# A second level of seven block products inside gate and up of an already Strassen-like MLP

## Chip, cores, metric

One Trainium2 chip, one core of it. The metric is the device time of one execution in microseconds (us). A ratio of two kernels is the mean time of one's fast runs over the mean time of the other's fast runs of the same rounds, so it is not quite the ratio of the medians that are quoted.

Engines: PE is the matrix engine (TensorE), DVE the vector engine, ACT the scalar engine, POOL the GpSimd engine. PEld in the profile is PE's loading of weights. SBUF is the on-chip memory that all engines read; PSUM holds PE's results, in banks of 512 f32 columns.

## The reference

Two layers, each a linear attention block (A) and a bilinear gated MLP (B), with a residual around both. Only B matters here:

```python
def _B_ref(x, w_gate, w_up, w_down):      # x (1, 2048, 1024), F = 3584
    g = jnp.einsum("bsd,df->bsf", x, w_gate)
    u = jnp.einsum("bsd,df->bsf", x, w_up)
    h = g * u
    return jnp.einsum("bsf,fd->bsd", h, w_down)
```

## The kernel before

All tensors of B lie in one big on-chip array, the "arena", so the profile calls every operand `arena` and every accumulator `ps` (PSUM). A small planner records each instruction with the bytes it reads and writes, and adds the semaphore waits.

B already replaces 2x2 block products by the seven products of the Strassen-Winograd scheme. A *unit* is a pair of 128-column feature tiles of gate (m = 0) or of up (m = 1), over 1024 tokens. Its seven products take 4 matmuls of 128x128 by 128x512 each, 28 instead of 32. There are 28 units in a *pass* (14 of gate, 14 of up), and two passes in each of the two layers: passes 1 to 4. After each pass comes the down projection of the same tokens.

```python
xs = {"1": (raw[:, 0:4, 0:128], rraw, xblk(0, s0), r_xblk(0, s0)),      # weights, activations
      "2": (raw[:, 4:8, 0:128], rraw, xblk(1, s0), r_xblk(1, s0)),
      "3": (sv[:, 3], rs[3], xblk(1, s0 + 512), r_xblk(1, s0 + 512)),
      "4": (raw[:, 4:8, 128:256], rraw, T4, rT[2]),
      "5": (sv[:, 0], rs[0], T1, rT[0]), ... }
def pe(q, bank, start):
    w, rw, x, rx = xs[q]
    P.add("pe", lambda e: [e.matmul(psb(bank), w[:, k, :], x[:, k, :], start=(start and k == 0), stop=(k == 3),
                                    skip_group_check=True) for k in range(4)], rd=rw + rx, pwr=[bank])
def fin(b, bank, ti):                                                   # a finished block of gate or up
    ...
    if ti is None:
        if m == 0: P.add("act", ... AF.Copy ...)                        # gate: ACT copies it out
        else:      stt(hv[:, j, :], psb(bank), SG, g4[b], gr, hr, prd=[bank], op1=ALU.mult)
    elif m == 0:
        stt(g4[b], psb(bank), SG, tm[ti][0], tm[ti][1], gr, prd=[bank])
    else:                                                               # up: add, then multiply with gate
        stt(ut, psb(bank), SG, tm[ti][0], tm[ti][1], ur, prd=[bank])    # DVE, one input in PSUM, one in SBUF
        tt(hv[:, j, :], ut, g4[b], ALU.mult, ur + gr, hr)               # DVE, both inputs in SBUF
...
```

`stt` is a DVE scalar_tensor_tensor, `tt` a DVE tensor_tensor.

## Time and profile before

The time is 1497.7 us (median of 4 runs, 1495.4 to 1498.2).

The first lines are from the page of the kernel before: the span, busy time with its share of the span, the chain of waits that ended last by engine, and the costliest group (busy us, mean ns of one, then the idle time before it).

```profile
span 1495.1 us, 17704 instructions
...
PE 1479.0 (99%) x6925; PEld 660.1 (44%) x6990; DVE 913.9 (61%) x1530; ACT 449.2 (30%) x732; POOL 216.0 (14%) x239
...
PE 91%; DVE 3%; DMA 3%; issue 1%; POOL 1%; ACT 1%; SPq 0%; ACTq 0%
...
L912 PE MATMUL ps<-arena 128*128 128x512 f16 x3136 | 679.0, 379 | 1.9 <-DVE arena L613 1.3
```

PE is busy throughout and the chain is PE: 679.0 us / 3136 = 216.5 ns per gate/up matmul. The mean of 379 ns in the line is one matmul from start to end; they overlap, and their starts in the trace lie 216 ns apart.

The next answer is the view of stretches, one row for each of the four passes, from the first gate/up matmul to the last: length, busy us of each engine with the number of instructions, granted PE clock, DMA share, GB/s.

```profile
core 0: us, PE busy (x) PEld busy (x) DVE busy (x) ACT busy (x) POOL busy (x), PEclk, DMA share, GB/s
243.10:415.70 172.60, 171.18 (x791) 73.42 (x791) 129.18 (x288) 66.70 (x113) 2.37 (x6) 1.00 0.83 253
499.00:669.50 170.50, 170.45 (x791) 73.44 (x791) 83.27 (x143) 66.11 (x112) 6.31 (x16) 1.00 0.72 207
983.70:1154.90 171.20, 170.58 (x790) 73.42 (x790) 74.25 (x125) 67.73 (x114) 2.36 (x6) 1.00 0.56 170
1238.20:1408.80 170.60, 170.55 (x791) 73.51 (x791) 68.69 (x111) 66.11 (x112) 0.00 (x0) 1.00 0.56 177
```

PE fills all four. DVE fills 75% of pass 1 and 40 to 49% of the others; POOL does next to nothing. The DVE line is its largest group of tensor_tensor with 512 elements and both inputs in SBUF, from the groups by line with shapes kept apart:

```profile
L610 DVE TENSOR_TENSOR arena<-arena 128x512 f16<-128x512 f16 x140 | 59.5, 425 | 4.8
```

### The profile page before, as it was taken

The page shows a single profiled execution, that of the slowest core. Times are in us where ns is not written, and L with a number is a line of the kernel's source. Part 1 is how long each engine was busy: PE and PEld are TensorE (multiplying, and loading weights), DVE is VectorE, ACT ScalarE, POOL GpSimd, SP SyncE. Part 2 cuts the span into 40 slices and gives each one's busy share as a digit, 9 for nine tenths or more (in the row PEclk, how much of TensorE's full clock was granted, in tenths as well). Part 3 has the DMA queues.
Part 4 walks back from the last instruction along what each step waited for, and adds up shares of the span by engine and source line. Part 5 has one row for each costly group of instructions (what it writes and reads, how often), then busy time and mean ns, then how long its engine had stood idle before and what let it go on. Part 6 is the DMA issues. An engine that isn't in the chain of part 4 may idle for free.

```text
span 1495.1 us, 17704 instructions
## 1 busy us (share of the span) xinstructions
PE 1479.0 (99%) x6925; PEld 660.1 (44%) x6990; DVE 913.9 (61%) x1530; ACT 449.2 (30%) x732; POOL 216.0 (14%) x239
## 2 busy tenths in 40 slices
PE   8999999999999999999999999999999999999999
PEld 4444444444444444444444444444444444444444
DVE  7986978777656463445488678764344553434453
ACT  3332355333300234330023314543333003334200
POOL 4544621000000010000044345310000000000000
PEclk9999999999999999999999999999999999999999
DMA  6134656799854896544466247555554455555352
GB/s 225 36 92 111 149 132 150 229 285 278 262 203 151 260 257 193 176 164 148 141 184 178 80 93 186 146 139 172 178 173 163 163 190 186 177 175 177 131 172 99
DMA packets 300643, 254.40 MB, mean 170 GB/s; under 512 B 102288, under 2 KB 266384, under 8 KB 300560
## 3 DMA queue, kind: packets, MB, share of 16 engines
q1 hardware_dynamic: 300560, 253.27, 57.4%
q8 instruction: 55, 0.90, 0.3%
q14 instruction: 28, 0.23, 0.0%
HBM read 195.04 MB, written 34.60 MB: 154 GB/s over the span
## 4 chain that ended last, share of the span: by engine, by line
PE 91%; DVE 3%; DMA 3%; issue 1%; POOL 1%; ACT 1%; SPq 0%; ACTq 0%
PE ps L912 43%; PE ps L1035 23%; PE ps L672 15%; PE ps L754 7%; PE ps L840 2%; DMA arena<-in_B_w_down_dram 1%; DVE arena L610 1%; DVE arena L412 1%; DMA arena<-arena 1%; DMA arena<-in_A_wqkv_dram 1%; POOL arena L701 1%; PE ps L766 0%; PE ps L794 0%; SPq L386 0%; POOL arena L417 0%
## 5 line engine op out<-in xcount | busy, mean ns | idle before, releaser
L912 PE MATMUL ps<-arena 128*128 128x512 f16 x3136 | 679.0, 379 | 1.9 <-DVE arena L613 1.3
L613 DVE SCALAR_TENSOR_TENSOR arena<-ps,arena 128x512 f16<-128x512 f32 (+2 forms) x480 | 327.2, 689 | 470.6 <-PE ps L912 161.8
L912 PEld LDWEIGHTS ps<-arena 128*128 128x128 f16 (+1 forms) x3136 | 291.4, 98 | 388.2 <-ACT arena L916 36.0
L1035 PE MATMUL ps<-arena 128*128 128x512 f16 (+1 forms) x1548 | 338.0, 379 | 1.1
L1035 PEld LDWEIGHTS ps<-arena 128*128 128x128 f16 x1568 | 153.5, 98 | 185.0
L672 PE MATMUL ps<-arena 128*128 128x512 bf16 x1003 | 222.1, 379 | 4.6 <-DMA arena<-in_A_wqkv_dram 1.6
L916 ACT ACTIVATE arena<-ps 128x512 f32<-128x512 f32 x224 | 133.7, 597 | 291.1 <-PE ps L912 288.9
L610 DVE TENSOR_TENSOR arena<-arena 128x512 f16<-128x512 f16 (+3 forms) x360 | 197.9, 574 | 18.3 <-DMA arena<-in_B_w_down_dram 8.3
L672 PEld LDWEIGHTS ps<-arena 128*128 128x128 f16 x1024 | 99.6, 98 | 122.4 <-DMA arena<-in_A_wqkv_dram 2.1
L558 ACT ACTIVATE arena<-ps 128x512 f32<-128x512 f32 x128 | 76.4, 597 | 232.6 <-PE ps L672 218.4
L938 ACT COPY ps<-ps 128x512 f32<-128x512 f32 x112 | 63.9, 570 | 204.3 <-PE ps L912 203.7
L754 PE MATMUL ps<-arena 128*128 128x512 bf16 x500 | 114.6, 379 | 0.6
L840 PE MATMUL ps<-arena 128*128 128x512 bf16 x502 | 110.8, 379 | 3.2 <-ACT ps L834 2.7
L415 POOL TENSOR_SCALAR arena<-arena 128x1 f32<-128x1 f32 x64 | 20.7, 323 | 598.7 <-DVE arena L414 598.7
L412 DVE BATCH_NORM_STATS2 arena<-arena 128x6 f32<-128x512 bf16 x128 | 88.1, 689 | 13.1 <-DMA arena<-in_A_x_dram 6.7
L701 POOL TENSOR_TENSOR arena<-arena 128x1024 f16<-128x1024 f32 x32 | 79.8, 2493 | 90.3 <-DVE arena L699 83.7
L926 ACT ACTIVATE arena<-ps 128x512 f16<-128x512 f32 x112 | 66.9, 597 | 84.5 <-PE ps L912 84.5
L561 DVE SCALAR_TENSOR_TENSOR arena<-ps,arena 128x512 bf16<-128x512 f32 x128 | 88.5, 692 | 4.4
L684 POOL TENSOR_TENSOR arena<-arena 128x512 f32<-128x512 f32 x60 | 74.6, 1248 | 87.0 <-DVE arena L561 85.6
L559 DVE TENSOR_SCALAR arena<-arena 128x512 f32<-128x512 f32 x128 | 65.9, 515 | 27.7 <-ACT arena L558 26.6
L840 PEld LDWEIGHTS ps<-arena 128*128 128x128 f16 x512 | 49.8, 98 | 63.9 <-ACT ps L834 4.4
L754 PEld LDWEIGHTS ps<-arena 128*128 128x128 f16 x512 | 49.3, 98 | 55.7
(45 smaller groups left out, 381.9 us busy)
## 6 DMA issues: line engine op xcount, KB each, us to landing
arena<-s_scratch SPq DMA_DIRECT2D x84, 512.0 KB, 3.3
arena<-in_B_w_gate_dram SPq DMA_DIRECT2D x56, 512.0 KB, 4.2
arena<-in_B_w_up_dram SPq DMA_DIRECT2D x56, 512.0 KB, 3.9
arena<-t_scratch SPq DMA_DIRECT2D x32, 896.0 KB, 4.8
arena<-in_B_w_down_dram SPq DMA_DIRECT2D x24, 896.0 KB, 4.6
s_scratch<-arena SPq DMA_DIRECT2D x28, 512.0 KB, 6.9
arena<-in_A_wqkv_dram SPq DMA_DIRECT2D x12, 1024.0 KB, 8.3
arena<-in_A_x_dram SPq DMA_DIRECT2D x31, 256.0 KB, 3.2
```

Source lines behind the costliest of these rows:

```text
L412: P.add("dve", (lambda h: lambda e: e.bn_stats(st[j][:, 6 * h:6 * h + 6], x_res[:, i, (D // 2) * h:(D // 2) * (h + 1)]))(h), rd=r_x(i, (D ...
L558: P.add("act", lambda e: e.activation(etmp[r], psb(bank), AF.Exp), prd=[bank], wr=er)
L561: P.add("dve", lambda e: e.scalar_tensor_tensor(out=dst_ap, in0=psb(bank), scalar=0.0, in1=etmp[r], op0=ALU.max, op1=ALU.add), prd=[bank], ...
L610: P.add("dve", lambda e: e.tensor_tensor(out=out, in0=a, in1=b, op=op), rd=rd, wr=wr, prd=prd)
L613: P.add("dve", lambda e: e.scalar_tensor_tensor(out=out, in0=a, scalar=sc, in1=b, op0=ALU.mult, op1=op1), rd=rd, wr=wr, prd=prd)
L672: return [e.matmul(psb(bank), xnT[:, k, i * 128:(i + 1) * 128], w[:, k, h * 512:(h + 1) * 512], start=(k == 0), stop=(k == KT - 1)) for k ...
L701: P.add("pool", lambda e: e.tensor_tensor(out=asb[b].rearrange("p (h c) -> p h c", c=32), in0=pbuf.rearrange("p (h c) -> p h c", c=32), in ...
L754: return [e.matmul(psb(bank), xr[:, t, j * 128:(j + 1) * 128], pk[:, h, t, :], start=(t == 0), stop=(t == NST - 1)) for t in range(NST)]
L840: return [e.matmul(psb(bank), xnT[:, g, i * 128:(i + 1) * 128], wp[:, g, dh * 512:(dh + 1) * 512], start=(dh == 0 and g == 0), stop=(g == ...
L912: P.add("pe", lambda e: [e.matmul(psb(bank), w[:, k, :], x[:, k, :], start=(start and k == 0), stop=(k == 3), skip_group_check=True) for k ...
L916: P.add("act", lambda e: e.activation(tm[i][0], psb(bank), AF.Copy, scale=SG), prd=[bank], wr=tm[i][1])
L1035: return [e.matmul(psb(bank), hv[:, 7 * hf + k, t * 128:(t + 1) * 128], w[:, k, :], start=(start and hf == 0 and k == 0), stop=(hf == 1 an ...
```

## The change

The intent is to take more off PE. Two units that share m become a pair A, B. In a chosen set of the seven products ("2", "3", "4"), the 4 + 4 matmuls of 512 columns are replaced by seven products of 2 matmuls of 256 columns, over the pair of feature tiles and the two halves of the 512 tokens. That is 14 x 256 instead of 8 x 512 columns, one 512-column matmul less per group. Cut to its core:

```diff
-    SG = 16.0
+    SG = 4.0
+    L2SETS = {(False, 0): "3", (False, 1): "234", (True, 0): "234", (True, 1): "234"}     # (second layer?, pass in layer)
+    PAIR_ORDER = "P1A 21 P1B D3A 26 P6A 27 S3= D3B 41 D2A P6B R T0 S2+ D2B 46 P7A 31 47 P7B D4A 36 D4B P5A 37 P5B T1 S4+"
...
+    def sums():                     # DVE: four weight sums per second-level product, 256 elements each
+        for o, a_, b_, op in (...):
+            tt(sp[:, o], a_[0], b_[0], op, a_[1] + b_[1], rp[o])
+    def acp(dst, rd_, bank):        # ACT: copies 256 columns out
+        P.add("act", lambda e: e.activation(dst, psb(bank)[:, 0:256], AF.Copy, scale=SG), prd=[bank], wr=rd_)
+    def padd(i, src, rsrc):         # POOL: combines partial results in SBUF, 256 elements of f32
+        P.add("pool", lambda e: e.tensor_tensor(out=ss[:, i], in0=ss[:, i], in1=src, op=ALU.add), rd=rss[i] + rsrc, wr=rss[i])
+    def st6():
+        mm(6, xk, 0, False); mm(5, yk, 0, True)
+        acp(ss[:, 1], rss[1], xk); acp(c5, rc5, yk); padd(1, c5, rc5)
+    def st7():
+        mm(7, xk, 0, False); acp(ss[:, 2], rss[2], xk)
+        P.add("pool", lambda e: e.tensor_tensor(out=ss[:, 3], in0=ss[:, 2], in1=c5, op=ALU.add), rd=rss[2] + rc5, wr=rss[3])
+    def fold_cp(c):                 # POOL, 512 elements of f32: product 3 also needs P1+P6
+        P.add("pool", lambda e: e.tensor_tensor(out=s_, in0=s_, in1=t, op=ALU.add), rd=r_ + r, wr=r_)
...                                  # (statements joined on a line here; much cut)
+    for k in range(4): stash(4 + k)  # four residual tiles are parked in DRAM; their place is scratch during a pass
```

With one, three, three and three products in the four passes and 14 pairs in each, there are 140 groups. Each brings four DVE sums and two short POOL adds, and product 3 two long POOL adds per pair besides. Products 2 and 4 also cost DVE more instructions when they are finished, because they now need an addend.

More of the change, by code (lines that the diff above doesn't have):

```diff
@@ L232, in build_kernel @@
     O_R = RB + 12288
-    O_TMP = O_R
     O_DRAW = O_R + 12288
@@ L246, in build_kernel @@
     O_YS = [RE + i * 2048 for i in range(2)]
-    O_G4 = RE
-    O_UT = [RE + 4096 + i * 1024 for i in range(2)]
+    O_UT = [RE + 6144, RB + 31744]
+    O_TP = {"3": RE, "2": RE + 3072, "4": RB + 28672}
+    O_CP = O_R
+    O_SS = [None, O_R + 8192]
+    O_C5 = [O_R + 14336, O_R + 15360]
     TOTAL = take(0)
@@ L320, in build_kernel @@
         rtmp = [vf(O_R + i * 2048, 512) for i in range(8)]
-        gtmp = [vf(O_TMP + i * 2048, 512) for i in range(6)]
         draw = vb(O_DRAW, 2048).rearrange("p (e c) -> p e c", c=D)
         dout = vh(O_DOUT, 2048).rearrange("p (q c) -> p q c", c=512)
-        g4 = [vh(O_G4 + i * 1024, 512) for i in range(4)]
         utmp = [vh(o, 512) for o in O_UT]
@@ L355, in build_kernel @@
         B_GY = [2, 3]
-        B_GZ = 4
-        B_DX = [5, 6, 7, 4]
+        B_GZ = [4, 7]
+        B_L2 = [5, 6]
+        B_DX = [7, 4, 5, 6]
         B_DV = [0, 2, 1, 3]
@@ L581, in build_kernel, with unit_jm @@
         DPROD = ["1", "2", "7", "4", "6", "5", "3"]
+        def unit_jm(u):
+            return 2 * (u // 4) + u % 2, u // 2 % 2
         def ring_issue():
@@ L591, in ring_issue @@
             if u < NU:
-                j, m = divmod(u, 2)
+                j, m = unit_jm(u)
                 raw = vb(o, 2048).rearrange("p (k c) -> p k c", c=256)
@@ L629, in t_ops, with tp_ops @@
                     lambda: tt(T4, b21, T2, ALU.subtract, r21 + rt2, rt4)]
+        def tp_ops(pair, prods):
+            s0 = pair * 1024
+            res = []
+            for q in prods:
+                if q == "4":
+                    x, base, st_ = T4, O_T + 8192, 1024
+                else:
+                    s1 = s0 + (512 if q == "3" else 0)
+                    x, base, st_ = xblk(1, s1), O_XT + 4 * S * 2 + s1 * 2, S * 2
+                o = O_TP[q]
+                tp = [vh(o + i * 1024, 512).rearrange("p (k s) -> p k s", s=256) for i in range(3)]
+                rt = [R(o + i * 1024, 1024) for i in range(3)]
+                b11, b12, b21, b22 = [x[:, 2 * k:2 * k + 2, 256 * c:256 * c + 256] for k in range(2) for c in range(2)]
+                r11, r12, r21, r22 = [_seg(base + 2 * k * st_, 2, st_, c * 512, (c + 1) * 512) for k in range(2) for c in range(2)]
+                res += [(lambda tp=tp, rt=rt, a=b12, b=b11, ra=r12, rb=r11: tt(tp[0], a, b, ALU.subtract, ra + rb, rt[0])),
+                        (lambda tp=tp, rt=rt, a=b22, ra=r22: tt(tp[1], a, tp[0], ALU.subtract, ra + rt[0], rt[1])),
+                        (lambda a=b22, b=b12, ra=r22, rb=r12: tt(b, a, b, ALU.subtract, ra + rb, rb)),
+                        (lambda tp=tp, rt=rt, a=b21, ra=r21: tt(tp[2], a, tp[1], ALU.subtract, ra + rt[1], rt[2]))]
+            return res
         def prep_s(n):
@@ L871, in layer_A @@
                 if nxt.t_next >= 8 and RG["tq"] is None:
-                    RG["tq"] = t_ops(0)
+                    RG["tq"] = t_ops(0) + tp_ops(0, L2SETS[not first, 0])
                 if RG["tq"]:
@@ L882, in layer_B @@
             lnp.need(7)
-            for f in t_ops(0) if RG["tq"] is None else RG["tq"]:
+            for f in t_ops(0) + tp_ops(0, L2SETS[not first, 0]) if RG["tq"] is None else RG["tq"]:
                 f()
@@ L887, in layer_B, with stash, pair @@
                 nxt.on_act = False
-            def unit(ps_, u):
-                n = ps_ * NPASS + u
-                m = u % 2
-                j = u // 2
+            def stash(i):
+                dma(xscr[i * 128:(i + 1) * 128, :], x_res[:, i, :], R(V_X + i * 32, 32), KXS[i], rd=r_x(i))
+            def pair(ps_, p, l2):
+                xp = O_X + (8 * ps_ + 4) * D * 2
+                m = p % 2
                 s0 = ps_ * 1024
-                o = r_slot(n)[0][0]
-                raw = vb(o, 2048).rearrange("p (k c) -> p k c", c=256)
-                sv = vh(o + 4096, 2048).rearrange("p (q k c) -> p q k c", q=4, c=128)
-                X, Y, Z = B_GX[u % 2], B_GY[u % 2], B_GZ
+                X, Y, Z = B_GX, B_GY, B_GZ
@@ L898, in unit @@
                 rT = [R(O_T + i * 4096, 4096) for i in range(3)]
-                rraw = R(o, 4096)
-                rs = [R(o + 4096 + i * 1024, 1024) for i in range(4)]
-                tm = [(gtmp[3 * m + i], R(O_TMP + (3 * m + i) * 2048, 2048)) for i in range(3)]
-                xs = {"1": (raw[:, 0:4, 0:128], rraw, xblk(0, s0), r_xblk(0, s0)),
-                      "2": (raw[:, 4:8, 0:128], rraw, xblk(1, s0), r_xblk(1, s0)),
-                      "3": (sv[:, 3], rs[3], xblk(1, s0 + 512), r_xblk(1, s0 + 512)),
-                      "4": (raw[:, 4:8, 128:256], rraw, T4, rT[2]),
-                      "5": (sv[:, 0], rs[0], T1, rT[0]),
-                      "6": (sv[:, 1], rs[1], T2, rT[1]),
-                      "7": (sv[:, 2], rs[2], xblk(0, s0 + 512), r_xblk(0, s0 + 512))}
@@ L910, in pe @@
-                def pe(q, bank, start):
-                    w, rw, x, rx = xs[q]
+                H = {"1": (hA, O_HA), "2": (hC, O_HC), "4": (hB, O_HB), "3": (hD, O_HD)}
+                o_sp = {"3": xp + 4096, "2": xp + 6144, "4": O_R + 12288}
+                o_ss = [xp, O_R + 8192]
+                units = []
+                for ab_ in range(2):
+                    n = ps_ * NPASS + 2 * p + ab_
+                    o = r_slot(n)[0][0]
+                    raw = vb(o, 2048).rearrange("p (k c) -> p k c", c=256)
+                    sv = vh(o + 4096, 2048).rearrange("p (q k c) -> p q k c", q=4, c=128)
+                    rraw = R(o, 4096)
+                    rs = [R(o + 4096 + i * 1024, 1024) for i in range(4)]
+                    units.append(dict(j=unit_jm(2 * p + ab_)[0], n=n, w={
+                        "1": (raw[:, 0:4, 0:128], rraw), "2": (raw[:, 4:8, 0:128], rraw), "3": (sv[:, 3], rs[3]), "4": (raw[:, 4:8, 128:256], rraw),
+                        "5": (sv[:, 0], rs[0]), "6": (sv[:, 1], rs[1]), "7": (sv[:, 2], rs[2])}))
@@ new lines, in pair, with cpb, pe @@
+                xb = {"1": (xblk(0, s0), r_xblk(0, s0)), "2": (xblk(1, s0), r_xblk(1, s0)), "3": (xblk(1, s0 + 512), r_xblk(1, s0 + 512)),
+                      "4": (T4, rT[2]), "5": (T1, rT[0]), "6": (T2, rT[1]), "7": (xblk(0, s0 + 512), r_xblk(0, s0 + 512))}
+                def cpb(i, c):
+                    o = O_CP + (2 * i + c) * 2048
+                    return vf(o, 512), R(o, 2048)
+                def pe(q, c, bank, start):
+                    (w, rw), (x, rx) = units[c]["w"][q], xb[q]
@@ L912, in pe, with cp @@
                     P.add("pe", lambda e: [e.matmul(psb(bank), w[:, k, :], x[:, k, :], start=(start and k == 0), stop=(k == 3),
                                                     skip_group_check=True) for k in range(4)], rd=rw + rx, pwr=[bank])
-                def cp(i, bank):
-                    P.add("act", lambda e: e.activation(tm[i][0], psb(bank), AF.Copy, scale=SG), prd=[bank], wr=tm[i][1])
-                H = [(hA, O_HA), (hC, O_HC), (hB, O_HB), (hD, O_HD)]
-                def fin(b, bank, ti):
-                    gr = R(O_G4 + b * 1024, 1024)
-                    hv, ho = H[b]
+                def cp(i, c, bank):
+                    t, r = cpb(i, c)
+                    P.add("act", lambda e: e.activation(t, psb(bank), AF.Copy, scale=SG), prd=[bank], wr=r)
@@ L923, in fin, with mul @@
+                def mul(c, dst, bank, add):
+                    hv, ho = H[dst]
+                    j = units[c]["j"]
                     hr = R(ho + j * 1024, 1024)
-                    if ti is None:
+                    hx = hv[:, j, :]
+                    if add is None:
                         if m == 0:
-                            P.add("act", lambda e: e.activation(g4[b], psb(bank), AF.Copy, scale=SG), prd=[bank], wr=gr)
+                            P.add("act", lambda e: e.activation(hx, psb(bank), AF.Copy, scale=SG), prd=[bank], wr=hr)
@@ L927, in fin @@
                         else:
-                            stt(hv[:, j, :], psb(bank), SG, g4[b], gr, hr, prd=[bank], op1=ALU.mult)
+                            stt(hx, psb(bank), SG, hx, hr, hr, prd=[bank], op1=ALU.mult)
                     elif m == 0:
-                        stt(g4[b], psb(bank), SG, tm[ti][0], tm[ti][1], gr, prd=[bank])
+                        stt(hx, psb(bank), SG, add[0], add[1], hr, prd=[bank])
                     else:
-                        ut, ur = utmp[b % 2], R(O_UT[b % 2], 1024)
@@ L933, in fin @@
-                        stt(ut, psb(bank), SG, tm[ti][0], tm[ti][1], ur, prd=[bank])
-                        tt(hv[:, j, :], ut, g4[b], ALU.mult, ur + gr, hr)
-                def part_p1():
-                    pe("1", X, True)
-                    P.add("act", lambda e: e.copy(psb(Z), psb(X)), prd=[X], pwr=[Z])
-                def part_p4():
-                    pe("4", X, False)
-                    fin(2, X, None)
-                def part_p26():
-                    pe("2", Z, False)
-                    fin(0, Z, None)
-                    pe("6", X, False)
-                    cp(1, X)
@@ L950, in part_p3 @@
-                def part_p3():
-                    pe("3", Y, False)
-                    fin(3, Y, 1)
-                def part_p5():
-                    pe("5", Y, True)
-                def part_p7():
-                    pe("7", X, False)
-                    cp(2, X)
-                    fin(1, Y, 2)
-                return part_p1, part_p4, part_p26, part_p3, part_p5, part_p7
-            def gateup(ps_, ticks):
-                prev = None
-                jit = first and ps_ == 0
-                units = [unit(ps_, u) for u in range(NU)]
-                for u in range(NU):
-                    n = ps_ * NPASS + u
-                    cur = units[u]
-                    if jit and u == 0:
-                        prep_s(n)
-                        prep_s(n + 1)
-                    if u != 1:
-                        cur[0]()
-                    if u == 1:
-                        cur[4]()
-                    if prev:
-                        prev[1]()
-                        cur[2]()
-                        prev[3]()
-                        ring_issue()
-                        if u != 1:
-                            cur[4]()
-                    else:
-                        cur[4]()
-                        cur[2]()
-                        units[1][0]()
-                    cur[5]()
-                    if jit:
-                        store_s(n)
-                        if u + 2 < NU:
-                            prep_s(n + 2)
-                    ticks(u)
-                    prev = cur
-                def tail():
-                    prev[1]()
-                    prev[3]()
@@ new lines, in mul, with p1, p6, p7 @@
+                        ut, ur = utmp[c], R(O_UT[c], 1024)
+                        stt(ut, psb(bank), SG, add[0], add[1], ur, prd=[bank])
+                        tt(hx, ut, hx, ALU.mult, ur + hr, hr)
+                def p1(c):
+                    pe("1", c, X[c], True)
+                    P.add("act", lambda e: e.copy(psb(Z[c]), psb(X[c])), prd=[X[c]], pwr=[Z[c]])
+                def p6(c):
+                    pe("6", c, X[c], False)
+                    cp(0, c, X[c])
+                def p7(c):
+                    pe("7", c, X[c], False)
+                    cp(1, c, X[c])
@@ new lines, in p5, with l2_of, mm, s_of @@
+                def p5(c):
+                    pe("5", c, Y[c], True)
+                    mul(c, "2", Y[c], cpb(1, c))
+                ORDER = [q for q in "243" if q in l2]
+                def l2_of(q):
+                    ci = len(ORDER) * p + ORDER.index(q)
+                    xk, yk = B_L2[ci % 2], B_L2[(ci + 1) % 2]
+                    so = o_ss[ci % 2] if len(ORDER) > 1 else o_ss[0]
+                    co = O_C5[ci % 2] if len(ORDER) > 1 else O_R + 8192
+                    sp = vh(o_sp[q], 1024).rearrange("p (i k c) -> p i k c", i=4, c=128)
+                    rp = [R(o_sp[q] + i * 512, 512) for i in range(4)]
+                    wA, rA = units[0]["w"][q]
+                    wB, rB = units[1]["w"][q]
+                    x, rx = xb[q]
+                    tp = [(vh(O_TP[q] + i * 1024, 512).rearrange("p (k s) -> p k s", s=256), R(O_TP[q] + i * 1024, 1024)) for i in range(3)]
+                    ss = vf(so, 1024).rearrange("p (c s) -> p c s", s=256)
+                    rss = [R(so + i * 1024, 1024) for i in range(4)]
+                    c5, rc5 = vf(co, 256), R(co, 1024)
+                    b11, b12, b21, b22 = [(x[:, 2 * k:2 * k + 2, 256 * c:256 * c + 256], rx) for k in range(2) for c in range(2)]
+                    qs = {1: ((wA[:, 0:2, :], rA), b11), 2: ((wA[:, 2:4, :], rA), b21), 3: ((sp[:, 3], rp[3]), b22), 4: ((wB[:, 2:4, :], rB), tp[2]),
+                          5: ((sp[:, 0], rp[0]), tp[0]), 6: ((sp[:, 1], rp[1]), tp[1]), 7: ((sp[:, 2], rp[2]), b12)}
+                    def sums():
+                        for o, a_, b_, op in ((0, (wB[:, 0:2, :], rB), (wB[:, 2:4, :], rB), ALU.add), (1, (sp[:, 0], rp[0]), (wA[:, 0:2, :], rA), ALU.subtract),
+                                              (2, (wA[:, 0:2, :], rA), (wB[:, 0:2, :], rB), ALU.subtract), (3, (wA[:, 2:4, :], rA), (sp[:, 1], rp[1]), ALU.subtract)):
+                            tt(sp[:, o], a_[0], b_[0], op, a_[1] + b_[1], rp[o])
+                    def mm(i, bank, half, start):
+                        (w, rw), (xx, rxx) = qs[i]
+                        P.add("pe", lambda e: [e.matmul(psb(bank)[:, 256 * half:256 * half + 256], w[:, k, :], xx[:, k, :], start=(start and k == 0),
+                                                        stop=(k == 1), skip_group_check=True) for k in range(2)], rd=rw + rxx, pwr=[bank])
+                    def acp(dst, rd_, bank):
+                        P.add("act", lambda e: e.activation(dst, psb(bank)[:, 0:256], AF.Copy, scale=SG), prd=[bank], wr=rd_)
+                    def padd(i, src, rsrc):
+                        P.add("pool", lambda e: e.tensor_tensor(out=ss[:, i], in0=ss[:, i], in1=src, op=ALU.add), rd=rss[i] + rsrc, wr=rss[i])
+                    def s_of(c):
+                        return vf(so + 2048 * c, 512), rss[2 * c] + rss[2 * c + 1]
+                    def st1():
+                        mm(1, xk, 0, True)
+                        acp(ss[:, 0], rss[0], xk)
+                    def st6():
+                        mm(6, xk, 0, False)
+                        mm(5, yk, 0, True)
+                        acp(ss[:, 1], rss[1], xk)
+                        acp(c5, rc5, yk)
+                        padd(1, c5, rc5)
+                    def st7():
+                        mm(7, xk, 0, False)
+                        acp(ss[:, 2], rss[2], xk)
+                        P.add("pool", lambda e: e.tensor_tensor(out=ss[:, 3], in0=ss[:, 2], in1=c5, op=ALU.add), rd=rss[2] + rc5, wr=rss[3])
+                    def direct(c, bank):
+                        if c == 0:
+                            mm(2, bank, 0, False)
+                            mm(3, bank, 1, False)
+                        else:
+                            mm(4, bank, 0, False)
+                    return dict(sums=sums, st1=st1, st6=st6, st7=st7, direct=direct, s=s_of)
@@ new lines, in pair, with fin @@
+                L = {q: l2_of(q) for q in ORDER}
+                def fold_cp(c):
+                    s_, r_ = L["3"]["s"](c)
+                    t, r = cpb(0, c)
+                    P.add("pool", lambda e: e.tensor_tensor(out=s_, in0=s_, in1=t, op=ALU.add), rd=r_ + r, wr=r_)
+                def fin(q, c):
+                    bank = {"2": Z, "4": X, "3": Y}[q][c]
+                    if q in L:
+                        L[q]["direct"](c, bank)
+                    else:
+                        pe(q, c, bank, False)
+                    add = L[q]["s"](c) if q in L else cpb(0, c) if q == "3" else None
+                    return lambda: mul(c, {"2": "1", "4": "4", "3": "3"}[q], bank, add)
@@ new lines, in pair, with gateup, step, sums @@
+                return dict(p1=p1, p5=p5, p6=p6, p7=p7, L=L, fin=fin, fold=fold_cp, units=units)
+            def gateup(ps_, ticks, l2):
+                jit = first and ps_ == 0
+                NP = NU // 2
+                pairs = [pair(ps_, p, l2) for p in range(NP)]
+                def step(p, q, i):
+                    L = pairs[p]["L"]
+                    if q in L:
+                        L[q]["st%d" % i]()
+                def sums(p, q):
+                    if p < NP and q in pairs[p]["L"]:
+                        pairs[p]["L"][q]["sums"]()
+                def fold(p, c):
+                    if "3" in l2:
+                        pairs[p]["fold"](c)
+                n0 = ps_ * NPASS
+                if jit:
+                    prep_s(n0)
+                    prep_s(n0 + 1)
+                for p in range(NP):
+                    c = pairs[p]
+                    if p == 0:
+                        for q in "24":
+                            if "S%s+" % q in PAIR_ORDER:
+                                sums(0, q)
+                    for tk in PAIR_ORDER.split():
+                        x = "AB".find(tk[-1])
+                        if tk[0] == "P":
+                            c["p" + tk[1]](x)
+                        elif tk[0] in "24":
+                            step(p, tk[0], int(tk[1]))
+                        elif tk[0] == "3":
+                            pp = p - 1 if tk[-1] == "'" else p
+                            if pp >= 0:
+                                step(pp, "3", int(tk[1]))
+                                if tk[1] != "1":
+                                    fold(pp, int(tk[1]) - 6)
+                        elif tk[0] == "D":
+                            pp = p - 1 if tk[1] == "3" else p
+                            if pp >= 0:
+                                pairs[pp]["fin"](tk[1], x)()
+                        elif tk == "R":
+                            if p:
+                                ring_issue()
+                                ring_issue()
+                        elif tk[0] == "S":
+                            sums(p + (tk[2] == "+"), tk[1])
+                        else:
+                            assert tk[0] == "T"
+                            i = int(tk[1])
+                            if jit:
+                                if i:
+                                    store_s(n0 + 2 * p)
+                                    store_s(n0 + 2 * p + 1)
+                                if p + 1 < NP:
+                                    prep_s(n0 + 2 * p + 2 + i)
+                            ticks(2 * p + i)
+                def tail():
+                    for tk in PAIR_ORDER.split():
+                        if tk[0] == "3" and tk[-1] == "'":
+                            step(NP - 1, "3", int(tk[1]))
+                            fold(NP - 1, int(tk[1]) - 6)
+                    for x in range(2):
+                        pairs[NP - 1]["fin"]("3", x)()
@@ L998, in tail @@
                     ring_issue()
+                    ring_issue()
+                    for t in range(4):
+                        i = 8 * ps_ + 4 + t
+                        dma(x_res[:, i, :], xscr[i * 128:(i + 1) * 128, :], r_x(i), KX[i], rd=R(V_X + i * 32, 32))
                 return tail
@@ L1078, in down @@
                         ticks(q, t)
-            def stash(i):
-                dma(xscr[i * 128:(i + 1) * 128, :], x_res[:, i, :], R(V_X + i * 32, 32), KXS[i], rd=r_x(i))
             if first:
@@ L1095, in ticks0 @@
             def ticks0(u):
-                if not lnp.done():
+                if u % 4 < 2 and not lnp.done():
                     lnp.flush_step()
@@ L1102, in dticks0 @@
             def dticks0(q, t):
-                if q in "6":
-                    tq[t]()
+                if q == "2" and t == 3:
+                    for k in range(4):
+                        stash(12 + k)
+                if q in "65":
+                    for _ in range(1 if q == "6" else 3):
+                        if tq:
+                            tq.pop(0)()
                 if q == "5" and t == 3 and not is_last:
@@ L1112, in ticks1 @@
             def ticks1(u):
-                if not is_last and nxt.t_next < 8:
+                if u % 4 < 2 and not is_last and nxt.t_next < 8:
                     nxt.step_t(1)
@@ L1138, in layer_B @@
                 wd_tick(0)
-            tail = gateup(0, ticks0)
+            for k in range(4):
+                stash(4 + k)
+            tail = gateup(0, ticks0, L2SETS[not first, 0])
             lnp.need(NST - 1)
-            tq = t_ops(1)
+            tq = t_ops(1) + tp_ops(1, L2SETS[not first, 1])
             down(0, dticks0, tail)
-            tail = gateup(1, ticks1)
+            tail = gateup(1, ticks1, L2SETS[not first, 1])
             down(1, dticks1, tail)
```

## The prediction

> **What bounds the kernel now.** TensorE. The page gives PE 1479.0 of 1495.1 us (99%), and the chain that ended last is 91% PE. Gate and up (matmul L912 in the groups by line) are 3136 matmuls of 512 columns, 679.0 us: 216.5 ns each, back to back. In the table of stretches each gate/up pass takes 166 to 170 us with PE waiting under 2 us. The Trainium skill ("TensorE: Matmul & The Clock Gate", "Wait — 56ns, not 53.3ns?") gives N/2.4 GHz + about 2.5 ns, 215.7 ns at 512; this trace agrees.
>
> **What changes.** Pairs of units share a second level: 8 matmuls of 512 columns become 14 of 256. The sets are 1, 3, 3 and 3 products over the four passes, 14 pairs each: 140 groups. Removed: 1120 x 216.5 ns = 242 us. Added: 1960 matmuls of 256 columns. The trace has none; by the same formula 109 ns each (estimate), 214 us. The 128-column matmuls (L766) take 12.4/128 = 97 ns, so the weight load should just hide under 256 columns. PE gain: about 28 us, 1.9%.
>
> **What it adds elsewhere** (estimates from durations in the trace, per pair of units with three products; PE then needs about 11.5 us instead of 12.13):
> - DVE: queued scalar_tensor_tensor cost about 0.63 us, 512-element tensor_tensor 0.376 (8 in 3.01), so 256-element ones about 0.24. Gate pairs: 8 of the first and 12 small sums, about 8 us. Up pairs: 8 dependent pairs at 1.1 us plus sums, about 11.8 us, as long as PE. DVE was 40 to 49% busy in the last three passes; after, 75 to 90%.
> - POOL: six 256-element and two 512-element adds (1.25 us each in L684), about 6 us of 11.5. The skill ("SBUF — State Buffer", "Who interferes with whom") says a DVE operation with two SBUF inputs contends with a GpSimd one that reads SBUF. The trace has a neighbouring case: the DVE tensor_scalar beside POOL adds has median 427 ns, longest 1209. So tensor_tensor will be stretched.
> - DMA: the same bytes, but the sums for the next pair come on DVE right after the ring is refilled, and need a load that lands about 4 us later (3.9 to 4.2 us for gate and up): DVE waits there.
> - Entry to the second layer's first pass: 12 more small tensor_tensor and the first sums before the products of the first pair: up to 5 us of PE wait, once.
>
> **On the critical path.** PE saves 28 us; DVE becomes nearly critical and gives part back: PE will wait for DVE to free PSUM banks in up pairs, about 0.3 to 1 us per two pairs (21 of them), 6 to 20 us, plus 2 to 5 us at the entry. Net gain about 13 us.
>
> **Prediction: 1485 us, 1470 to 1502 in 8 of 10.** Faster by over 2%: 0.03; within 2%: 0.92; slower by over 2%: 0.05.
>
> **What would show it.** 256-column matmuls at 108 to 112 ns in bulk; PE busy down 25 to 28 us; PE waits on DVE L613/L610-like lines up from 1.3 to 10 to 20 us, mostly in up pairs of passes 2 to 4; DVE tensor_tensor means above their lone durations and POOL busy up by roughly 300 us; pass 1 down by about 3 us only.
>
> **What would make it wrong.** Weight loads not hidden at 256 columns (each 10 ns costs 20 us); DVE stretched by POOL far more than assumed, making passes DVE-bound and the kernel slower; or all DVE work hiding, giving about 1470.

## More of the kernel before

In pass 1 DVE also prepares the weight sums `sv` of every unit (stored, and loaded in the later passes) and the sums of the down weights. That is why pass 1 is DVE's fullest stretch.

## The result, and the profile after

The kernel after takes 1522.6 us (median of 4, 1518.3 to 1522.9), ratio 1.0163 (1.0142 to 1.0183): 25 us slower. It lies outside the predicted range.

Page of the kernel after:

```profile
span 1520.9 us, 21573 instructions
...
PE 1474.7 (97%) x7765; PEld 749.3 (49%) x7830; DVE 1227.1 (81%) x2298; ACT 571.0 (38%) x1208; POOL 581.6 (38%) x631
...
PE 66%; DVE 24%; issue 4%; DMA 2%; ACT 2%; POOL 2%; SPq 0%; DVEq 0%; ACTq 0%
...
L1055 POOL TENSOR_TENSOR arena<-arena 128x512 f32<-128x512 f32 x112 | 151.1, 1349 | 8.8
```

PE's busy time fell by 4 us only, and the chain is now 24% DVE. "Busy" hides a part: one matmul takes 379 ns from start to end while the next starts after 216, so each wait between matmuls also leaves about 0.16 us more inside the busy time. The starts are clearer. In this trace 256-column matmuls start 109 ns apart (median of 1960), 512-column ones 216. So I take for each pass the time from its first to its last gate/up matmul, and subtract 215.8 ns for each 512-column matmul and 109 ns for each 256-column one. The rest is what PE lost:

| pass | before: matmuls, lost | after: matmuls, lost |
|---|---|---|
| 1 | 170.5, 2.0 | 167.7, 23.3 |
| 2 | 170.5, 0.0 | 162.1, 16.0 |
| 3 | 170.5, 0.8 | 162.1, 13.2 |
| 4 | 170.5, 0.0 | 162.1, 4.5 |
| sum | 682.0, 2.8 | 654.0, 57.0 |

The matmuls shrank by 28.0 us, as predicted; the time lost between them grew by 54.2 us. The difference, 26.2, is the change of the span (25.8) within the error of this count. Everything outside the passes is as before: from a pass's last gate/up matmul to the next first one, 83 us of down projection and 314 us with block A.

The same stretches after:

```profile
243.00:433.90 190.90, 175.16 (x874) 85.99 (x874) 162.09 (x346) 84.41 (x169) 61.01 (x62) 0.96 0.80 242
517.10:695.20 178.10, 168.62 (x1043) 97.82 (x1043) 169.53 (x365) 100.66 (x252) 107.22 (x128) 1.00 0.65 196
1009.60:1184.90 175.30, 169.09 (x1043) 99.89 (x1043) 166.22 (x356) 101.74 (x254) 102.92 (x118) 0.98 0.56 168
1268.10:1434.60 166.50, 165.29 (x1042) 99.17 (x1042) 157.35 (x333) 100.51 (x252) 100.31 (x112) 1.00 0.57 178
```

DVE is busy for 85% of pass 1 and 94 to 95% of the other three. POOL went from nothing to 60% of passes 2 to 4. And the clock: it was at half for three windows of 6.8 us (two in pass 1, one at the start of pass 3). The starts of the matmuls in them lie 2.7, 2.5 and 2.9 us further apart in sum than at 216 and 109 ns: about 8 of the 57 us.

DVE's tensor_tensor groups by shape:

```profile
L616 DVE TENSOR_TENSOR arena<-arena 128x512 f16<-128x512 f16 x264 | 144.6, 555 | 8.0
L616 DVE TENSOR_TENSOR arena<-arena 128x256 f16<-128x256 f16 x308 | 114.8, 403 | 4.9
...
L616 DVE TENSOR_TENSOR arena<-arena 128x256 f16<-128x256 bf16 x252 | 83.5, 359 | 0.8 <-DMA arena<-in_B_w_gate_dram 0.8
```

This is what I should have feared. The same 512-element f16 instruction took 425 ns before and takes 555 on average now. Here the tensor_tensor of 512 and 256 elements and the scalar_tensor_tensor of the whole trace are sorted by how they overlap in time a POOL tensor_tensor of 256 or 512 f32 elements, a "POOL add" (counted from the packed trace, all instructions):

| DVE instruction | no overlap: count, mean ns | a POOL add starts during it: count, mean ns | it starts during a POOL add: count, mean ns, longest |
|---|---|---|---|
| tensor_tensor, 512 (f16, bf16), both inputs in SBUF | 225, 420 | 44, 425 | 135, 772, 1507 |
| tensor_tensor, 256 (f16, bf16), both inputs in SBUF | 363, 283 | 78, 285 | 119, 750, 1319 |
| scalar_tensor_tensor, one f32 input in PSUM, one in SBUF | 339, 688 | 116, 680 | 237, 684, 693 |

Only those with two SBUF inputs are longer, and only when the POOL add started first. The timeline of pass 1 (start, length, engine, line, instruction, count, idle before) shows how it becomes a wait of PE:

```profile
302.36 6.43 DVE L616 TENSOR_TENSOR arena<-arena 128x512 f16<-128x512 f16 x9
302.79 0.92 POOL L1021 TENSOR_TENSOR arena<-arena 128x256 f32<-128x256 f32 x1 [7.54 <-ACT arena L1018]
...
303.79 1.32 POOL L1055 TENSOR_TENSOR arena<-arena 128x512 f32<-128x512 f32 x1
...
308.71 1.28 DVE L619 SCALAR_TENSOR_TENSOR arena<-ps,arena 128x512 f16<-128x512 f32 x2
...
309.45 0.61 PE L1014 MATMUL ps<-arena 128*128 128x256 f16 x4 [2.54 <-DVE arena L619]
```

Nine short tensor_tensor in a row take 6.43 us, 0.71 each, where eight of them took 3.01 before. Inside that row the single starts and lengths are:

```
302.36 DVE 0.43   302.70 DVE 0.42   303.15 DVE 0.83   303.91 DVE 1.48   305.32 DVE 0.94   306.18 DVE 1.48   307.69 DVE 0.43 ...
                  302.79 POOL 0.92           303.79 POOL 1.32   305.07 POOL 0.91   306.06 POOL 1.32
```

In this row every DVE instruction that starts during a POOL add ends only about 0.3 us after that add does, and the next POOL add has begun by then. PE stands for 2.54 us until DVE frees its bank.

The waits of PE in pass 1 (its two largest) and in pass 2 (waiting for, us in total, times, longest):

```profile
PE ps L947 <- DVE arena L619: 7.8, 2, 4.0
PE ps L1014 <- DVE arena L619: 6.0, 5, 2.5
...
PE ps L1014 <- ACT arena L1018: 4.6, 7, 0.9
PE ps L947 <- DVE arena L619: 3.6, 6, 1.0
```

In pass 1 PE waits for DVE itself. In pass 2 the larger part is a wait for ACT's copies of 256 columns, and these copies (L1018) in turn wait there for DVE's scalar_tensor_tensor, 19 times, 20.4 us in all: there the delay of DVE reaches PE by way of ACT.

### The profile page after: what moved, and what is told of

Same layout as the page of the kernel before. It is cut to its first block, busy times and chain, and to the rows that moved or that the text cites. A ratio compares the mean times of both kernels' runs of the same rounds, so it can differ in the third digit from the quotient of the medians.

```text
span 1520.9 us, 21573 instructions
## 1 busy us (share of the span) xinstructions
PE 1474.7 (97%) x7765; PEld 749.3 (49%) x7830; DVE 1227.1 (81%) x2298; ACT 571.0 (38%) x1208; POOL 581.6 (38%) x631
## 4 chain that ended last, share of the span: by engine, by line
PE 66%; DVE 24%; issue 4%; DMA 2%; ACT 2%; POOL 2%; SPq 0%; DVEq 0%; ACTq 0%
PE ps L1176 22%; PE ps L947 15%; PE ps L698 14%; DVE arena L616 9%; DVE arena L619 8%; PE ps L1014 7%; PE ps L780 5%; DVE arena L415 2%; PE ps L866 2%; DVE arena L718 1%; DVE arena L721 1%; DMA arena<-arena 1%; DMA arena<-in_B_w_down_dram 1%; ACT arena L1018 1%; POOL arena L727 1%
## 5 line engine op out<-in xcount | busy, mean ns | idle before, releaser
L619 DVE SCALAR_TENSOR_TENSOR arena<-ps,arena 128x512 f16<-128x512 f32 (+2 forms) x564 | 376.0, 684 | 180.6 <-PE ps L1176 141.8
L947 PE MATMUL ps<-arena 128*128 128x512 f16 x2016 | 503.7, 383 | 13.7 <-DVE arena L619 11.6
L616 DVE TENSOR_TENSOR arena<-arena 128x256 f16<-128x256 f16 (+5 forms) x1044 | 481.7, 499 | 20.0 <-DMA arena<-arena 3.4
L1014 PE MATMUL ps<-arena 128*128 128x256 f16 x1960 | 285.9, 275 | 18.7 <-DVE arena L619 6.0
L947 PEld LDWEIGHTS ps<-arena 128*128 128x128 bf16 (+1 forms) x2016 | 197.0, 99 | 183.3 <-DVE arena L619 19.1
L1021 POOL TENSOR_TENSOR arena<-arena 128x256 f32<-128x256 f32 x140 | 105.2, 751 | 394.6 <-ACT arena L1018 394.6
L1014 PEld LDWEIGHTS ps<-arena 128*128 128x128 f16 (+1 forms) x1960 | 183.5, 98 | 142.2 <-ACT arena L1018 27.5
L1176 PEld LDWEIGHTS ps<-arena 128*128 128x128 f16 x1568 | 153.4, 98 | 184.2
L1018 ACT ACTIVATE arena<-ps 128x256 f32<-128x256 f32 x560 | 193.2, 384 | 103.8 <-PE ps L1014 58.1
L698 PEld LDWEIGHTS ps<-arena 128*128 128x128 f16 x1024 | 100.1, 98 | 122.0 <-issue 1.8
L1055 POOL TENSOR_TENSOR arena<-arena 128x512 f32<-128x512 f32 x112 | 151.1, 1349 | 8.8
L1040 POOL TENSOR_TENSOR arena<-arena 128x256 f32<-128x256 f32 x140 | 110.5, 789 | 63.6 <-ACT arena L1018 63.6
L710 POOL TENSOR_TENSOR arena<-arena 128x512 f32<-128x512 f32 x60 | 74.7, 1249 | 87.3 <-DVE arena L564 85.9
```

Source lines behind the costliest of these rows:

```text
L616: P.add("dve", lambda e: e.tensor_tensor(out=out, in0=a, in1=b, op=op), rd=rd, wr=wr, prd=prd)
L619: P.add("dve", lambda e: e.scalar_tensor_tensor(out=out, in0=a, scalar=sc, in1=b, op0=ALU.mult, op1=op1), rd=rd, wr=wr, prd=prd)
L698: return [e.matmul(psb(bank), xnT[:, k, i * 128:(i + 1) * 128], w[:, k, h * 512:(h + 1) * 512], start=(k == 0), stop=(k == KT - 1)) for k ...
L1014: P.add("pe", lambda e: [e.matmul(psb(bank)[:, 256 * half:256 * half + 256], w[:, k, :], xx[:, k, :], start=(start and k == 0), stop=(k == ...
L1018: P.add("act", lambda e: e.activation(dst, psb(bank)[:, 0:256], AF.Copy, scale=SG), prd=[bank], wr=rd_)
L1055: P.add("pool", lambda e: e.tensor_tensor(out=s_, in0=s_, in1=t, op=ALU.add), rd=r_ + r, wr=r_)
```

## Experiments

**Theories.** A: POOL's reads of SBUF hold up DVE's two-input instructions, DVE falls behind, and PE waits. B: DVE simply has too many new instructions, whatever POOL does. C: the new schedule (pair order, ring slots held longer, parked tiles, scale) costs the time. The check against the reference passed in all runs, also where the result was wrong on purpose: presumably the MLP adds too little to the residual here for it to see such errors. Those kernels are for timing only.

"Lost" in the table is as above, per pass, from the trace of each run; "ratio" is to the kernel before.

| run | edit of after | us | ratio | lost in pass 1, 2, 3, 4 |
|---|---|---|---|---|
| e1_none | no second level | 1503.6 | 1.0045 | 7.5, 0.0, 1.0, 0.0 |
| e2_pass1_none | none in pass 1 | 1511.5 | 1.0097 | 7.9, 16.2, 11.6, 4.3 |
| e3_pool_noread | POOL adds become memsets | 1476.0 | 0.9861 | 2.6, 0.7, 7.2, 0.3 |
| e4_sums_once | weight sums for one pair only | 1494.6 | 0.9979 | 22.1, 0.3, 6.1, 0.3 |
| e5_both | both | 1475.3 | 0.9854 | 2.4, 0.3, 6.1, 0.3 |
| e6_only3 | pass 1 none, then "3" | 1495.7 | 0.9994 | 7.8, -0.1, -0.1, -0.1 |
| e7_34 | pass 1 none, then "34" | 1489.1 | 0.9946 | 7.1, 1.0, 2.1, 0.8 |
| e8_24 | pass 1 none, then "24" | 1508.0 | 1.0071 | 7.4, 5.9, 10.3, 5.9 |
| e9_34_cp2 | e7 and a second copy buffer in pass 1 | 1482.7 | 0.9902 | 1.7, 1.2, 2.2, 1.0 |
| e10_long_noread | only the long POOL adds become memsets | 1487.1 | 0.9931 | 5.9, 10.1, 7.1, 0.3 |
| e11_short_noread | only the short ones | 1498.9 | 1.0013 | 10.0, 8.1, 10.1, 4.4 |
| e12_before_pool | before, with idle POOL adds | 1510.2 | 1.0087 | 17.3, 0.0, 0.0, 0.0 |

### Is it the schedule, the reads of POOL, or DVE's load?

**e1_none**

```diff
-    L2SETS = {(False, 0): "3", (False, 1): "234", (True, 0): "234", (True, 1): "234"}
+    L2SETS = {(False, 0): "", (False, 1): "", (True, 0): "", (True, 1): ""}
```

> No second level in any pass, all else of the change kept (pair order, two units' slots held, scale 4, stashed residual tiles). Theories A (DVE stretched by POOL's reads) and B (DVE has too much to do, whatever POOL does) both expect the time of before, 1494 to 1502 us, with all gate/up matmuls of 512 columns at 216 ns. Rival C (the new order and the longer held ring slots cost the time) expects over 1508 us.

Measured: 1503.6 us, between the two expectations. Passes 2 to 4 are as before, so the schedule itself is harmless there: C falls for them. Pass 1 loses 5.5 us more than before. PE's waits in pass 1 name an ACT copy:

```profile
PE ps L947 <- ACT arena L952: 6.4, 4, 1.8
```

That is taken up in e9. It need not be part of after's loss: e3, with the schedule of after, loses 2.6 us in pass 1.

**e3_pool_noread.** Each POOL add is replaced by two memsets of the same tile, with the same declared reads and writes; the same is done to the other two adds.

```diff
-    P.add("pool", lambda e: e.tensor_tensor(out=ss[:, i], in0=ss[:, i], in1=src, op=ALU.add), rd=rss[i] + rsrc, wr=rss[i])
+    for _ in range(2):
+        P.add("pool", lambda e: e.memset(ss[:, i], 0.5), rd=rss[i] + rsrc, wr=rss[i])
```

> Wrong result on purpose: each POOL add of the second level becomes two memsets of the same tile, so POOL waits for and releases the same things, is busy about as long, but reads no SBUF. DVE keeps every instruction. In the trace of after, DVE tensor_tensor that overlap a POOL add are stretched by about 103 us in all, and PE lost 54 us between matmuls. A expects DVE tensor_tensor back at 285 and 425 ns and 1475 to 1490 us. B expects the durations to matter little: 1508 us or more. C expects 1515 or more.

Measured: 1476.0 us, 46.6 below after, 1.4% faster than before. Passes and DVE groups of this run:

```profile
243.50:413.80 170.30, 168.45 (x875) 85.02 (x875) 142.88 (x346) 84.37 (x169) 48.91 (x118) 1.00 0.87 271
497.00:659.70 162.70, 162.43 (x1042) 100.65 (x1042) 145.51 (x365) 100.82 (x252) 88.43 (x240) 1.00 0.72 215
973.80:1143.10 169.30, 165.32 (x1043) 101.80 (x1043) 140.85 (x356) 101.70 (x254) 83.50 (x230) 0.98 0.57 174
1226.30:1388.60 162.30, 162.25 (x1042) 100.82 (x1042) 132.07 (x333) 100.50 (x252) 80.70 (x224) 1.00 0.58 183
```

```profile
L616 DVE TENSOR_TENSOR arena<-arena 128x512 f16<-128x512 f16 x264 | 110.2, 424 | 8.0
...
L616 DVE TENSOR_TENSOR arena<-arena 128x256 f16<-128x256 f16 x308 | 79.3, 287 | 4.9
```

POOL is still busy for half of passes 2 to 4, DVE executes as many instructions as in after (2298), and yet the tensor_tensor are back at 424 and 287 ns. Those that start during a memset are no longer than the others (125 of 512 elements, 424 ns; 177 of 256, 286 ns). DVE's busy time in the passes falls from 655 to 561 us, and 46.2 of the 57.0 us lost are gone. A holds. B as a sole cause, and C, fall. What remains is mostly the entry to pass 3 (7.2 us), where PE waits for the sums that DVE has to make first, of activations and weights (a row of 21 tensor_tensor in after); after and e5 have the same waits:

```profile
PE ps L1014 <- DVE arena L616: 3.9, 2, 2.6
```

**e4_sums_once** and **e5_both**

```diff
-                    if p < NP and q in pairs[p]["L"]:
+                    if p == 0 and q in pairs[p]["L"]:
                         pairs[p]["L"][q]["sums"]()
```

> Wrong result on purpose: the four weight sums of each second-level product are made only for the first pair of each pass, POOL adds as in after. It takes 520 DVE tensor_tensor away, 148 us at their lone duration and some 56 us of stretch. B expects 1472 to 1482 us, since DVE falls to about 1020 us busy. A expects part of that: the products of gate and up are still stretched beside POOL (about 30 us) and pass 1 still has its preparations, 1485 to 1500 us. C expects 1515 or more.

> Wrong result on purpose: both edits at once. If matmuls of 256 columns run at 109 ns as read in the trace of after, and nothing but DVE and POOL delays PE, this is PE's floor: 1468 to 1475 us. If something else (DMA, ACT copies, semaphore waits of groups of two matmuls) holds PE too, it stays above 1482.

e4 took 1494.6 us:

```profile
244.10:433.90 189.80, 176.12 (x875) 86.62 (x875) 151.72 (x294) 84.37 (x169) 61.76 (x61) 0.96 0.80 245
517.10:679.40 162.30, 162.25 (x1042) 100.79 (x1042) 120.27 (x209) 100.51 (x252) 106.00 (x128) 1.00 0.73 215
993.70:1161.90 168.20, 164.24 (x1042) 101.36 (x1042) 112.26 (x200) 101.57 (x254) 102.46 (x118) 0.99 0.57 175
1245.10:1407.50 162.40, 162.35 (x1043) 100.84 (x1043) 103.40 (x177) 100.52 (x252) 100.17 (x112) 1.00 0.57 183
```

This qualifies A. Without the sums, passes 2 to 4 lose nothing but the entry to pass 3 (6.1), although POOL adds as before: DVE then fills 64 to 74% of them. So in these three passes the stretch costs time only because DVE was nearly full with its own new work, and the new work only because it was stretched; taking away either is enough. Pass 1 has few sums, and there the reads alone make the loss (22.1 with, 2.6 without). e5 took 1475.3 us, in the lower expected range but for its last digit, and the trace agrees with the 109 ns. It loses 9.2 us in all, so DMA, ACT copies and the waits of short matmul groups cost little further. 6 to 7 us at the entry to pass 3 stand in all three runs; before it was 0.8.

### Where does DVE have room?

**e2_pass1_none, e6_only3, e7_34, e8_24.** Only `L2SETS` changes:

```diff
+    L2SETS = {(False, 0): "", (False, 1): "234", (True, 0): "234", (True, 1): "234"}    # e2
+    L2SETS = {(False, 0): "", (False, 1): "3",   (True, 0): "3",   (True, 1): "3"}      # e6
+    L2SETS = {(False, 0): "", (False, 1): "34",  (True, 0): "34",  (True, 1): "34"}     # e7
+    L2SETS = {(False, 0): "", (False, 1): "24",  (True, 0): "24",  (True, 1): "24"}     # e8
```

> A correct kernel: only pass 1 loses its one second-level product, passes 2 to 4 keep three. In the traces pass 1 stood 23.3 us above its matmuls in after and 7.5 in the run without any second level; its matmuls cost 2.8 us more without it. If pass 1's loss is POOL's reads holding up DVE's preparations, this takes 13 us off after: 1507 to 1512 us, with two of the three half-clock stretches gone. If the loss of pass 1 has another cause (loads of the down weights, say), 1518 or more.

> Correct: no second level in pass 1, one product (3) in passes 2 to 4. POOL then has two 256-element and two 512-element adds per pair, DVE 4 sums. PE's matmuls shrink by 8.4 us against before, pass 1 costs 5.5 more. If DVE has room once it isn't nearly full, no time is lost in passes 2 to 4 although POOL still reads: 1493 to 1498 us. If POOL's reads cost PE time in proportion to their number, passes 2 to 4 lose 10 us and it takes over 1502.

> Correct: none in pass 1, products 3 and 4 in passes 2 to 4. Matmuls save 16.8 us against before, pass 1 costs 5.5 more. With room on DVE: 1486 to 1491 us. If the loss goes with the number of POOL adds, over 1498.

> Correct: none in pass 1, products 2 and 4 in passes 2 to 4: as many matmuls as with 3 and 4, but no 512-element adds on POOL (four 256-element ones per pair), and more DVE products. Also room for PE: 1486 to 1491 us, a little below the run with 3 and 4 if the long POOL adds hurt most, above it if DVE's own work does.

e2, e6 and e7 came as theory A expects. In e7 DVE's 256-element tensor_tensor are stretched to 407 ns on average, some to 1357, and passes 2 to 4 still lose only 1 to 2 us each: stretch where there is slack costs next to nothing. e6 has as many long POOL adds and shows no stretch at all (285 ns). Of its tensor_tensor 42 do overlap an add, but 21 of them started before it, and the other 21 in its last 0.15 us; they take 424 and 427 ns. What counts is how the two fall in time, not the number of adds.

e8 missed. It has as many matmuls as e7 and no stretch (287 and 422 ns), yet it is 18.9 us slower. PE's waits in its pass 2:

```profile
PE ps L1014 <- ACT arena L952: 3.5, 14, 0.3
```

14 visible waits, one per pair, for an ACT copy of 512 columns. With the 0.16 us more that each leaves inside the busy time they make 5.8 us, which is all that the pass lost (5.9). Without product 3's short matmuls in between, a bank's copy probably isn't hidden any more; that is read from one trace and was not tested. It is a second way to lose the gain, unrelated to POOL.

### Which adds hurt, and do they hurt alone?

**e10_long_noread** replaces only `fold_cp`'s add by memsets, **e11_short_noread** only the other two (edits as in e3).

> Wrong result on purpose: of after's POOL adds only the 112 long ones (512 elements, 1.35 us) become memsets; the 280 short ones stay. If a DVE instruction waits for the whole POOL instruction, the harm goes with length squared: the long ones are 55% of it, all of it in pass 1, where they catch DVE's preparations. Expected 1485 to 1497 us, with pass 1 back to about 171 us and passes 2 to 4 still losing some. If all POOL adds harm alike by number: 1505 or more.

> Wrong result on purpose: the 280 short POOL adds become memsets, the 112 long ones stay. By length squared pass 1 stays near 190 us and passes 2 to 4 recover a good part: 1492 to 1505 us, above the run with the long ones removed. By number: 1485 or less.

112 adds of 1.3 us weigh more than 280 of 0.77 us: without the long ones 1487.1 us, without the short ones 1498.9, which is 0.32 us for each long add removed and 0.08 for each short one. The two kinds also stand at different places of the schedule, so length is not shown to be the only reason. In pass 4 the long ones are the whole loss (0.3 without them, 4.4 with them). Both runs lie in the range that the length rule gave. Its detail for pass 1 was too strict: e11's pass 1 lost 10.0 us, not over 20, so the long adds alone do less there than all adds together.

**e12_before_pool** puts POOL adds that nobody needs into the kernel before (and one memset of their tile at the start, not shown):

```diff
                     P.add("act", lambda e: e.activation(tm[i][0], psb(bank), AF.Copy, scale=SG), prd=[bank], wr=tm[i][1])
+                    for h in range(2):
+                        P.add("pool", lambda e, h=h: e.tensor_tensor(out=vf(RE + 6144, 256), in0=vf(RE + 6144, 256), in1=tm[i][0][:, 256 * h:256 * h + 256], op=ALU.add),
+                              rd=R(RE + 6144, 1024) + tm[i][1], wr=R(RE + 6144, 1024))
```

> The kernel before with 448 POOL adds of 256 elements that nobody needs, two after each ACT copy in gate and up (some 300 us of POOL, as in after). Theory: POOL's reads cost only where DVE has no slack. DVE tensor_tensor in gate and up are stretched here too, but DVE is 40 to 75% busy: 1496 to 1503 us, what is lost lies in pass 1. If POOL's reads cost time by themselves (PE or ACT slowed, or every stretch counted): 1512 or more.

Measured: 1510.2 us, more than I expected, but just where I expected it. Passes of this run and its 512-element group:

```profile
242.30:430.10 187.80, 174.16 (x791) 73.94 (x791) 152.56 (x288) 66.69 (x113) 87.58 (x118) 0.99 0.77 232
513.40:683.90 170.50, 170.45 (x791) 73.44 (x791) 90.18 (x143) 66.11 (x112) 90.25 (x128) 1.00 0.72 207
999.00:1169.50 170.50, 170.45 (x791) 73.43 (x791) 79.66 (x122) 66.94 (x114) 85.87 (x118) 1.00 0.56 170
1252.80:1423.30 170.50, 170.45 (x791) 73.44 (x791) 74.75 (x111) 66.11 (x112) 83.38 (x112) 1.00 0.56 177
```

```profile
L611 DVE TENSOR_TENSOR arena<-arena 128x512 f16<-128x512 f16 x140 | 85.1, 608 | 4.8
```

The products of gate and up are stretched in all four passes (608 ns mean). Passes 2 to 4, with DVE at 44 to 53%, lose 0.0 us. Pass 1, where DVE was 75% busy, loses 17.3, 15.3 more than before. PE's waits in pass 1 are for DVE above all, and ACT waits for POOL nowhere in pass 1, so the delay doesn't come by the copies' buffers that the added adds read:

```profile
PE ps L913 <- DVE arena L614: 11.0, 8, 2.5
PE ps L913 <- ACT ps L942: 2.6, 3, 1.3
```

So POOL's reads alone make in pass 1 a loss of the size of the change's (15.3 us more than before, against 21.3) in a kernel that has nothing else of the change; the adds are not the same ones, 112 short ones here where after has 28 short and 28 long.

### The version that the runs point to

**e9_34_cp2** is e7, and in pass 1 the copies of P1+P6 alternate between two buffers:

```diff
                 def cpb(i, c):
                     o = O_CP + (2 * i + c) * 2048
+                    if not l2 and i == 0 and p % 2:
+                        o = O_R + 8192 + c * 2048
```

> Correct; the version the runs point to. As the run with products 3 and 4 in passes 2 to 4, and pass 1's copies of P1+P6 alternate between two buffers, because in the traces without a second level PE waits there four times, 1.9 us each, for an ACT copy whose buffer DVE still reads. If that is pass 1's loss of 5.5 us against before: 1482 to 1486 us. If not: 1488 to 1490.

Measured: 1482.7 us, ratio 0.9902 (0.9887 to 0.9917), correct.

```profile
242.80:415.00 172.20, 170.86 (x790) 74.68 (x790) 130.29 (x288) 66.71 (x113) 2.37 (x6) 1.00 0.89 269
498.30:664.40 166.10, 166.05 (x958) 91.83 (x958) 133.18 (x281) 92.38 (x210) 86.31 (x100) 1.00 0.69 210
978.50:1145.50 167.00, 165.92 (x958) 91.96 (x958) 128.63 (x268) 93.25 (x212) 82.17 (x90) 1.00 0.58 178
1228.70:1394.60 165.90, 165.85 (x959) 92.09 (x959) 122.33 (x249) 92.39 (x210) 79.57 (x84) 1.00 0.57 180
```

Pass 1 is back at its old length, which confirms the buffer as e1's loss (7.1 in e7 to 1.7; the "1.9 us each" of the expectation are 1.5 to 1.8 in e1's trace). Passes 2 to 4 each take 4 to 5 us less than before, with DVE at 74 to 80%. It beats both kernels, by 14 us and by 40.

## Why the prediction was wrong, point by point

- *"PE gain: about 28 us"*, at 109 ns per 256-column matmul: right. 28.0 us, and e5 turns 21.7 us of it into time, the rest being its own waits. My argument for it was partly wrong: busy time divided by count gave 97 ns for 128-column matmuls, but their starts lie 56 ns apart. They come in groups of 4, and the last of each group adds its whole 219 ns to the busy time, so the weight load was not as near the limit as I wrote.
- *"PE will wait for DVE to free PSUM banks in up pairs, about 0.3 to 1 us per two pairs (21 of them), 6 to 20 us"*: this is the step that failed. The mechanism was right in the main (in pass 2 the wait often came by way of ACT), and so was its cause, POOL's reads beside two-input DVE instructions. But I named the stretch, and listed it among what would make the forecast wrong, without ever putting it in the sum. The same 964 tensor_tensor of 256 and 512 elements take 432 us in after and 330 in e3: 102 us on DVE, in passes where I had left it 10 to 25% of slack. PE's added loss was 54 us.
- *"pass 1 down by about 3 us only"*: wrong, it rose by 18 us. I looked for DVE pressure only where the three-product sets were, and passed over the one stretch in which DVE was already 75% busy. e12 shows that POOL reads alone cost 15 us there.
- *"DVE 75 to 90%"* after: 85% in pass 1, 94 to 95% in the others. Without the stretch, in e3, it is 81 to 89% in passes 2 to 4: the count of instructions was right, their length was not. *"POOL busy up by roughly 300 us"*: 366, as the adds take longer than I assumed (256 elements: 0.77 us on average where my sum had about 0.58; 512 elements: 1.35 us, where block A's take 1.25).
- *"up to 5 us of PE wait, once"* at the entry of the second layer: about right, 6.1 us in e4 and e5, of which 3.9 are the waits for DVE and about 1.5 a window of half clock.
- *"DVE waits there"* for the ring's load before the next pair's sums: not seen as a cost. In all of after the listed waits of DVE's tensor_tensor on the gate and up loads are 0.8 us.
- Not foreseen at all: waits of up to 4 us also bring PE's clock to half for a window, about 8 us of the loss. The Trainium skill ("TensorE: Matmul & The Clock Gate", "What's actually happening") gives an idle window of about 3.4 us as the trigger; this trace agrees only in kind: its halved windows begin within PE waits of 3.9, 4.0 and 2.6 us, and in the 3.4 us before them PE had been idle for 2.6, 2.3 and 2.2 us, not for all of it; in e11 2.0 us were enough. They last 6.8 us here and 3.4 in e11.

What stays open: how much of the 8 us of half clock would be lost all the same if the waits stayed but the clock didn't fall, and the ACT wait of e8, which was read and not tested.

## What to carry to other kernels

Before moving work to POOL because it idles, list the DVE instructions with two SBUF inputs in the same stretch, and add to each that may start during a POOL add the rest of that add (here up to 1.2 us). The f32 tensor_scalar of block A belongs on the list too: in before, the 27 that start during an add take 856 ns on average, the others 424. The short POOL adds hurt less than the long ones here. The price was paid where DVE was near full even without the stretch (75% of pass 1 in before, 81 to 89% of passes 2 to 4 in e3) and hardly where it was not, so look at DVE's share stage by stage and not at its mean. A PE saving of 2% is best taken in the part that DVE can follow: here two of three products in three of four passes gave 0.5%, and 1.0% with the second copy buffer; the full change cost 1.6%.

## What the Trainium skill lacked or had wrong

- "SBUF — State Buffer", "Who interferes with whom": its rule that a DVE instruction with two SBUF inputs contends with a GpSimd one that reads SBUF, not with one that only writes, is borne out (tensor_tensor of 512 elements that start during an add 772 ns, during a memset 424; scalar_tensor_tensor with a PSUM input 684 during an add, 688 alone). So is its word that the order decides which of the two is held up (tensor_tensor that started before the add: 425). It lacks how long a DVE instruction that was held up still takes once the add has ended: a median of 0.28 us for 512 elements and 0.15 for 256, about 0.14 us less than alone, so that a start in the last 0.15 us of an add costs nothing (e6, 21 of 21). With two busy queues this makes DVE instructions of 0.42 us take 0.83 to 1.48 us, one after the other.
- "TensorE: Matmul & The Clock Gate", "Back-to-back issue gap": its sustained figures for pairs of weight load and matmul, about 81 ns at 128 columns and 131 ns at 512, don't hold here. Each matmul with its own weights starts 56, 109 and 216 ns after the one before at 128, 256 and 512 columns, which is that section's own N/2.4 + 2.5.
- The same page, "What's actually happening": an idle window of about 3.4 us is more than was needed; the clock fell although PE had been idle for only 2.0 us of the 3.4 us before (e11), or for 2.2 to 2.6 us (the kernel after).
- No page was found to warn that busy time divided by count overstates the spacing of matmuls in short groups: 12.4 us / 128 = 97 ns against 56 ns between starts.
